# Attention and channel-mix kernel on one core: instruction order from a list schedule inside the kernel, shared PSUM banks, k and q transposed in fp32

## Chip, cores and metric

One core of a Trainium2 chip runs the kernel. The metric is the device time of one execution in microseconds (us). TensorE is PE below, VectorE DVE, ScalarE ACT, GpSimd POOL and SyncE SP.

## What is computed

Attention over 4 batches, 8 heads, 768 positions and 64 elements per head. A query sees its own and the 127 keys before it, and the first four keys of the sequence (the sinks). What comes out is the input x of a channel mix with two gates of its own:

```
scores = q @ k.T / 8, kept where 0 <= i - j < 128 or j < 4
a = softmax(scores);  x = a @ v                     # (4, 768, 512)
xk = mu_k * x + (1 - mu_k) * x_prev                 # x_prev: the position before
xr = mu_r * x + (1 - mu_r) * x_prev
out = sigmoid(xr @ w_r) * (relu(xk @ w_k) ** 2 @ w_v)
```

Inputs and output are fp32 (w_k 512x1024, w_v 1024x512, w_r 512x512); matmuls run in bf16.

## The kernel before, in words

The work is cut into 12 tiles of 256 positions (u = 0 to 11; three tiles, T = 0 to 2, make a batch). A tile goes through these steps, which the texts below call by these names:

- load: k, q and v of a tile. The first three tiles come as fp32 through SP's queue. From the fourth on, k and q are cast to bf16 on the way by DMAs that POOL issues (names kb, qb, L76); v stays fp32 (vs) and is cast by POOL (L179).
- preparation (`prepare`): four groups of four transposes each on PE (L172), k and q, two halves; ACT copies each group out of PSUM (L175).
- scores (L218) for each of four pairs of heads, exponential on ACT (L222), mask on DVE (L228, L231), values (L244, L255), division on DVE (L259, L260), which gives x. T > 0 has also a group of sink scores (L202).
- x transposed (L275), copied by ACT (L279), and mixed by DVE to xk and xr (L294, L298).
- the channel mix of a tile (`ffn`): eight key groups of four matmuls (L311) with relu on ACT and square on DVE, two gate groups (L323), four product groups (L331) with w_v, the last operation on DVE (L336) and the store (L339).

PE's order is written out by hand: a loop over n = 4u + c takes the pair c of tile u, and puts up to three pieces of an earlier tile's channel mix between its parts (`fill`). The other engines' order is made by the framework's scheduler. `idle` puts matmuls on zeros into PE's order in the first 18 us, 35 in all. PSUM has four pools: two banks for scores, two for transposes and sink scores, one for values, three for the channel mix. The weights come as fp32; POOL casts w_k and w_r to bf16 (L366, L369), DVE w_v (L372).

Of the kernel before, what the change touches and what calls it, by code (L numbers as in the profile page):

```python
# [8 lines left out]
FP32 = mybir.dt.float32  # L9
# [4 lines left out]
PSUM = bass.MemoryType.PSUM  # L14


@with_exitstack
def kernel(
# [14 lines left out]
    nc = tc.nc  # L33
# [25 lines left out]
    raw = {}  # L59

    def dtype(u, name):

        return FP32 if u < 3 or name == "v" else BF16

    def load(u, names="kqv", halves=1):
        b, T = divmod(u, NT)
        for name in names:
            if (u, name) not in raw:
                raw[u, name] = ld.tile([128, 2, H, D], dtype(u, name), name=name + ("s" if dtype(u, name) == FP32 else "b"))
        n = H // halves  # L70
        for i in range(halves):
            for name in names:
                for g in range(2):
                    s0 = 256 * T + 128 * g
                    ahead = dtype(u, name) != FP32
                    ins = (nc.gpsimd if ahead else nc.sync).dma_start(  # L76
                        out=raw[u, name][:, g, n * i:n * i + n, :],
                        in_={"k": k, "q": q, "v": v}[name][
                            b, n * i:n * i + n, s0:s0 + 128, :].rearrange("h p d -> p h d"))
                    if ahead:  # L80
                        tc.keep_in_program_order(ins)

    wk32 = const.tile([128, NC, Dff], FP32, name="wk32")
    wr32 = const.tile([128, NC, Dm], FP32, name="wr32")
    wv32 = const.tile([128, NF, Dm], FP32, name="wv32")
    with tc.manual_schedule(engines={mybir.EngineType.SP}):
        load(0, "kq", 2)
        load(0, "v")
        nc.sync.dma_start(out=wk32, in_=moe_w_k.rearrange("(c p) f -> p c f", p=128))
        load(1, "kq")  # L90
        nc.sync.dma_start(out=wr32, in_=moe_w_r.rearrange("(c p) f -> p c f", p=128))
        load(1, "v")
        nc.sync.dma_start(out=wv32, in_=moe_w_v.rearrange("(c p) f -> p c f", p=128))  # L93
        load(2)


    warm = const.tile([128, 512], BF16, name="warm")
    nc.vector.memset(warm, 0.0)
    ident32 = const.tile([128, 128], FP32, name="ident32")
    make_identity(nc, ident32)  # L100
    ident = const.tile([128, 128], BF16, name="ident")
    nc.gpsimd.tensor_copy(out=ident, in_=ident32)


    mask = const.tile([128, 2, 2, 2, 128], BF16, name="mask")
    mask0 = const.tile([128, 2, 3, 128], BF16, name="mask0")
# [9 lines left out]
    nc.gpsimd.memset(mask0, 1.0)  # L116
    keep(mask0[:, :, 0, :], "D")
    keep(mask0[:, :, 1, :], "U")
    keep(mask0[:, :, 2, :], "D")
    nc.gpsimd.memset(mask0[0:NS, :, 0:2, :], 1.0)  # L120

    wk_sb = const.tile([128, NC, Dff], BF16, name="wk_sb")
    wr_sb = const.tile([128, NC, Dm], BF16, name="wr_sb")
    wv_h = const.tile([128, NF, Dm], BF16, name="wv_h")
    mu_k_sb = const.tile([128, NC], FP32, name="mu_k_sb")
    nc.scalar.dma_start(out=mu_k_sb, in_=moe_mu_k.rearrange("(c p) -> p c", p=128))
    mu_r_sb = const.tile([128, NC], FP32, name="mu_r_sb")
    nc.scalar.dma_start(out=mu_r_sb, in_=moe_mu_r.rearrange("(c p) -> p c", p=128))

    nc.gpsimd.memset(mask, 1.0)  # L130
    for a in range(2):
        keep(mask[:, a, :, 0, :], "U")
        keep(mask[:, a, :, 1, :], "D")

    v_bufs = [const.tile([128, 2, H, D + 1], BF16, name=f"v{i}") for i in range(3)]
    for t in v_bufs:
        nc.gpsimd.memset(t[:, :, :, D:D + 1], 1.0)

    xts = [const.tile([128, NC, S + 2], BF16, name=f"xt{i}") for i in range(2)]
    for t in xts:  # L140
        nc.gpsimd.memset(t[:, :, 0:2], 0.0)

    ksink = [const.tile([128, NP * 136], BF16, name=f"ksink{i}") for i in range(2)]
    vsink = [const.tile([128, H, D + 1], BF16, name=f"vsink{i}") for i in range(2)]
    for t in ksink + vsink:
        nc.gpsimd.memset(t, 0.0)
# [337 lines left out]
```

## Time and profile before

| | |
|---|---|
| time, median of 3 runs | 205.57 us (205.5 to 205.82) |
| time of the profiled execution | 205.31 us |
| its span | 203.6 us |
| busy: PE, DVE, ACT, POOL | 180.9, 142.5, 125.2, 68.0 us |
| mean granted clock of PE | 0.966 |

The profile is of one execution. Its span runs from the first to the last instruction; its own time is 1.71 us longer. Busy time of PE counts matmuls from start to modelled end, and they overlap, so a busy PE is not PE at its peak. A clock of 1.00 is 2.4 GHz, 0.50 is 1.2 GHz.

### The profile page before, as it was taken

Reading aid. Unit: us, or ns where it says so; the run is one execution under the profiler, and the core shown is the slowest. Engines: PE = TensorE matmul, PEld = TensorE weight load, DVE = VectorE, ACT = ScalarE, POOL = GpSimd, SP = SyncE. Lnnn points to the kernel's source line nnn. Section 1 sums busy time; section 2 is a strip of 40 time slices with the busy share of each in tenths; the row PEclk is TensorE's granted clock in tenths of the full one; section 3 lists DMA queues with packets and bytes.
Section 4 is the critical chain, followed back from the end, with each engine's and each line's share of the span. In section 5 each row is a group of like instructions: output and inputs, shape, how many; then the busy total and the mean of one; then the engine's idle time right before and its main releaser. Section 6 shows DMA issues by size and latency. Waiting matters only on the chain.

```text
span 203.6 us, 4309 instructions
## 1 busy us (share of the span) xinstructions
PE 180.9 (89%) x1681; PEld 115.9 (57%) x1704; DVE 142.5 (70%) x345; ACT 125.2 (61%) x201; POOL 68.0 (33%) x106
## 2 busy tenths in 40 slices
PE   7976869853998999999998999999999999999992
PEld 2633636531584665665855656666647567566650
DVE  0079486950776995986878959858969688698731
ACT  2443527541586586795875785967857868756340
POOL 8947160172149922002389420031890000000000
PEclk9999669996699999999999999999999999999999
DMA  6999999879969999205299992002996011020202
GB/s 117 230 392 212 281 292 279 164 106 166 245 118 127 201 217 67 104 2 131 78 103 181 234 104 106 0 3 106 80 107 125 3 56 48 3 103 3 101 2 103
DMA packets 81572, 25.97 MB, mean 128 GB/s; under 512 B 76432, under 2 KB 76432, under 8 KB 81552
## 3 DMA queue, kind: packets, MB, share of 16 engines
q1 hardware_dynamic: 43056, 20.98, 41.2%
q0 software_dynamic: 37440, 4.72, 36.3%
q8 instruction: 13, 0.21, 0.4%
q10 hardware_dynamic: 1056, 0.00, 0.3%
q14 instruction: 7, 0.06, 0.1%
HBM read 24.12 MB, written 6.29 MB: 149 GB/s over the span
## 4 chain that ended last, share of the span: by engine, by line
PE 37%; DVE 20%; SPq 17%; DMA 10%; ACT 8%; issue 5%; POOL 2%; DVEq 0%; ACTq 0%
SPq L76 13%; PE mm L311 12%; DMA kb<-in_k_dram 8%; PE mm L323 8%; PE mm L331 7%; DVE o_sb L336 5%; DVE xk L298 5%; ACT e L222 4%; ACT kt L175 3%; DVE xr L298 2%; SPq L93 2%; DMA vs<-in_v_dram 2%; PE tps L172 2%; PE o L255 2%; DVE e L228 2%
## 5 line engine op out<-in xcount | busy, mean ns | idle before, releaser
L311 PE MATMUL mm<-xk,wk_sb 128*128 128x256 bf16 x384 | 52.1, 277 | 3.2 <-DVE xk L298 3.1
L222 ACT ACTIVATE e<-sc 128x1024 bf16<-128x1024 f32 (+1 forms) x48 | 45.9, 956 | 10.9 <-PE sc L218 10.1
L331 PE MATMUL mm<-wv_h,kk 128*128 128x512 bf16 x182 | 47.7, 385 | 1.0 <-DVE wv_h L372 0.3
L228 DVE TENSOR_TENSOR e<-e,mask 128x1024 bf16<-128x1024 bf16 x32 | 22.1, 690 | 28.9 <-ACT e L222 28.9
L315 ACT ACTIVATE rl<-mm 128x512 bf16<-128x512 f32 x48 | 28.9, 603 | 20.8 <-PE mm L311 17.6
L311 PEld LDWEIGHTS <-wk_sb 128*128 128x128 bf16 x384 | 35.2, 99 | 10.5 <-issue 5.0
L179 POOL CAST v<-vs 128x512 bf16<-128x512 f32 x24 | 18.5, 788 | 56.4 <-PE o L255 30.8
L298 DVE SCALAR_TENSOR_TENSOR xk<-td,mu_k_sb,xt 128x256 bf16<-128x256 bf16 x48 | 26.1, 578 | 0.0
L331 PEld LDWEIGHTS <-kk 128*128 128x128 bf16 x192 | 16.7, 99 | 14.0 <-issue 1.3
L323 PE MATMUL mm<-wr_sb,xr 128*128 128x512 bf16 x84 | 22.1, 380 | 0.7 <-issue 0.2
L298 DVE SCALAR_TENSOR_TENSOR xr<-td,mu_r_sb,xt 128x256 bf16<-128x256 bf16 x48 | 22.4, 499 | 0.0
L316 DVE TENSOR_TENSOR kk<-rl 128x512 bf16<-128x512 bf16 x48 | 20.0, 417 | 3.1 <-ACT rl L315 3.1
L255 PE MATMUL o<-v,e 128*128 128x65 bf16 x352 | 20.6, 194 | 1.1 <-DVE e L231 1.0
L255 PEld LDWEIGHTS <-e 128*128 128x128 bf16 x352 | 17.7, 98 | 5.9 <-DVE e L231 1.8
L260 DVE TENSOR_TENSOR x<-o,rec 128x256 bf16<-128x256 f32 x48 | 20.1, 420 | 0.7
L231 DVE TENSOR_TENSOR e<-e,mask 128x768 bf16<-128x768 bf16 x16 | 10.3, 641 | 14.8 <-ACT e L222 14.7
L336 DVE SCALAR_TENSOR_TENSOR o_sb<-th,mm 128x512 f32<-128x512 f32 x24 | 16.3, 679 | 4.0 <-PE mm L331 4.0
L175 ACT COPY kt<-tps 128x512 bf16<-128x512 bf16 x18 | 10.5, 583 | 13.9 <-PE tps L172 13.9
L218 PE MATMUL sc<-qt,kt 64*128 64x128 bf16 (+1 forms) x256 | 18.5, 244 | 0.0
L175 ACT COPY qt<-tps 128x512 bf16<-128x512 bf16 x18 | 10.5, 583 | 9.5 <-PE tps L172 9.5
L218 PEld LDWEIGHTS <-kt 64*128 64x128 bf16 x256 | 8.7, 95 | 13.3 <-issue 10.9
L76 POOL DMA_DIRECT2D qb<-in_q_dram x18 | 16.0, 907 | 0.0
(56 smaller groups left out, 211.4 us busy)
## 6 DMA issues: line engine op xcount, KB each, us to landing
vs<-in_v_dram SPq DMA_DIRECT2D x24, 256.0 KB, 5.2
out_dram<-o_sb SPq DMA_DIRECT2D x24, 256.0 KB, 2.0
kb<-in_k_dram POOLq DMA_DIRECT2D x18, 128.0 KB, 5.0
qb<-in_q_dram POOLq DMA_DIRECT2D x18, 128.0 KB, 5.8
wk<-in_moe_w_k_dram SPq DMA_DIRECT2D x1, 2048.0 KB, 9.4
wv<-in_moe_w_v_dram SPq DMA_DIRECT2D x1, 2048.0 KB, 13.6
ks<-in_k_dram SPq DMA_DIRECT2D x4, 256.0 KB, 10.1
qs<-in_q_dram SPq DMA_DIRECT2D x4, 256.0 KB, 5.9
```

What stands on the lines that cost most here:

```text
L76: ins = (nc.gpsimd if ahead else nc.sync).dma_start(out=raw[u, name][:, g, n * i:n * i + n, :], in_={"k": k, "q": q, "v": v}[name][b, n * ...
L175: nc.scalar.copy(out=dst[:, 2 * half:2 * half + 2, :, :], in_=ps)
L218: nc.tensor.matmul(out=sc[:, a, o0:o1], lhsT=lhs[rows], rhs=rhs[rows], start=True, stop=True)
L222: nc.scalar.activation(out=e[:, :, lo:], in_=sc[:, :, lo:], func=AF.Exp, scale=scale)
L228: nc.vector.tensor_tensor(out=e, in0=e, in1=mask.rearrange("p a g k q -> p a (g k q)"), op=ALU.mult)
L255: nc.tensor.matmul(out=o[:, g, a, :], lhsT=e[:, a, e0:e0 + 128], rhs=rhs, start=(T == 0 and i == 0), stop=(i == len(blocks) - 1), skip_gro ...
L298: nc.vector.scalar_tensor_tensor(out=dst[:, c0 + i, :], in0=td[:, i, :], scalar=mu[:, c0 + i:c0 + i + 1], in1=prv[:, i, :], op0=ALU.mult, ...
L311: nc.tensor.matmul(out=ps[:, i, :], lhsT=wk_sb[:, c, 128 * f:128 * f + 128], rhs=xk[:, c, :], start=(c == 0), stop=(c == NC - 1), skip_gro ...
L315: nc.scalar.activation(out=rl, in_=ps, func=AF.Relu)
L323: nc.tensor.matmul(out=ps, lhsT=xr[:, c, 128 * g:128 * g + 128], rhs=wr_sb[:, c, :], start=(c == 0), stop=(c == NC - 1))
L331: nc.tensor.matmul(out=ps, lhsT=kk[:, f, 128 * g:128 * g + 128], rhs=wv_h[:, f, :], start=(f == 0), stop=(f == NF - 1))
L336: nc.vector.scalar_tensor_tensor(out=o_sb, in0=th[g], scalar=1.0, in1=ps, op0=ALU.add, op1=ALU.mult)
```

## The change

A class `Plan` takes every operation of the kernel with its engine, an assumed length, what it reads and writes, which buffers it takes and holds, and a rank. `schedule` then goes through a model of the engines and always emits the operation that can start first; the rank decides between equals. All engines and SP's queue follow this order. Further: PSUM is one pool of six banks for all uses beside the two banks of scores; k and q of all tiles come as fp32 through SP's queue and are transposed in fp32 (no DMA is issued by POOL any more); DVE casts w_k and w_r; of the 35 idle matmuls 8 are left. The core of the diff:

```diff
+class Plan:
...
+    def op(self, engine, cost, emit, rank, reads=(), writes=(), take=(), hold=(), port=False,
+           lag=None, service=0.0):
+        self.ops.append(dict(engine=engine, cost=cost, emit=emit, rank=rank, reads=list(reads),
+                             writes=list(writes), take=list(take), hold=list(hold), port=port,
+                             lag=90.0 if lag is None else lag, service=service))
+
+    def schedule(self):
+        ops = self.ops
...
+            best = None
+            for engine, some in ready.items():
+                now = clock.get(engine, 0.0)
+                pick = None
+                for i in some:
+                    o = ops[i]
+                    t = max(now, at[i])
+                    if o["port"]:
+                        t = max(t, port.get("DVE" if engine == "POOL" else "POOL", 0.0))
+                    ok = True
+                    for name, _ in o["take"]:
+                        if not free[name]:
+                            ok = False
+                            break
+                        t = max(t, min(free[name])[0])
+                    if not ok:
+                        continue
+                    if pick is None or (t, o["rank"], i) < (pick[0], ops[pick[1]]["rank"], pick[1]):
+                        pick = (t, i)
+                if pick is None:
+                    continue
+                t0 = pick[0]
+                if best is None or t0 < best[0]:
+                    best = (t0, pick[1])
...
+            clock[o["engine"]] = t + o["cost"]
+            if o["port"]:
+                port[o["engine"]] = t + o["cost"]
+            end = t + o["cost"] + o["lag"]
+            if o["service"]:
...
-    ld = ctx.enter_context(tc.tile_pool(name="ld", bufs=3))
...
-    sc_ps = ctx.enter_context(tc.tile_pool(name="sc_ps", bufs=1, space=PSUM))
-    tr_ps = ctx.enter_context(tc.tile_pool(name="tr_ps", bufs=2, space=PSUM))
-    o_ps = ctx.enter_context(tc.tile_pool(name="o_ps", bufs=1, space=PSUM))
-    mm_ps = ctx.enter_context(tc.tile_pool(name="mm_ps", bufs=3, space=PSUM))
...
-        return FP32 if u < 3 or name == "v" else BF16
...
+    pool("sc", 1, [128, 2, 512], FP32, psum)
+    pool("bank", 6, [128, 512], FP32, psum)
...
-                    ins = (nc.gpsimd if ahead else nc.sync).dma_start(
...
+                    nc.sync.dma_start(
+                        out=buf[key][:, g, h0:h1, :],
+                        in_=src[b, h0:h1, s0:s0 + 128, :].rearrange("h p d -> p h d"))
...
+    for u in range(2, U):
+        load(u, "kqv", -92 if u == 2 else 10 * u - 18)
...
+    for i in range(4):
+        sl = slice(256 * i, 256 * i + 256)
+        P.op("DVE", dve(1024, 0.52), lambda sl=sl: nc.vector.tensor_copy(
+            out=wk_sb[:, :, sl], in_=wk32[:, :, sl]), 2 + i, reads=["wk32"], writes=[("wk", i)],
+            port=True)
+    for i in range(2):
+        P.op("DVE", dve(1024, 0.52), lambda i=i: nc.vector.tensor_copy(
+            out=wr_sb[:, 2 * i:2 * i + 2, :], in_=wr32[:, 2 * i:2 * i + 2, :]), 8 + i,
+            reads=["wr32"], writes=[("wr", i)], port=True)
+
...
+                        nc.tensor.transpose(
+                            out=ps[:, i, g, :],
+                            in_=src[:, g, 2 * c:2 * c + 2, :].rearrange("p a d -> p (a d)"),
+                            identity=ident if by else ident32)
+
+            P.op("PE", 250.0 if by else 450.0, transpose, rank + half, lag=PE_LAG,
+                 take=[("bank", psk)], reads=["ident" if by else "ident32"] + made, writes=[psk],
...
+                P.op("PE", 445.0, keys, rank + f2, lag=PE_LAG,
+                     take=[] if i else [("bank", psk)], hold=[("xk", u)] + ([psk] if i else []),
+                     reads=[("wk", f // 2)] + [("xk", u, c) for c in range(NC)] +
+                     ([psk + (0,)] if i else []), writes=[psk + (i,)])
...
+    idle(8, -200, ("idle", 0))
+    prepare(0, 0)
+    for u in range(U):
+        attend(u, 10 * u + 4)
+        if u + 1 < U:
+            prepare(u + 1, 10 * u + 11)
+        mix(u, 10 * u + 8)
+        if u > 0:
+            ffn(u - 1, 10 * u + FFN_AFTER)
+    ffn(U - 1, 10 * U + FFN_AFTER)
+    with tc.manual_schedule():
+        P.run()
...
-    def weights_k():
-        for i in range(4):
-            sl = slice(256 * i, 256 * i + 256)
-            nc.gpsimd.tensor_copy(out=wk_sb[:, :, sl], in_=wk32[:, :, sl])
-
-    def weights_rv():
-        nc.gpsimd.tensor_copy(out=wr_sb, in_=wr32)
-
-        for i in range(4):
-            nc.vector.tensor_scalar(out=wv_h[:, 2 * i:2 * i + 2, :],
-                                    in0=wv32[:, 2 * i:2 * i + 2, :],
-                                    scalar1=0.5, scalar2=None, op0=ALU.mult)
...
-                    prepare(u + 1, *PARTS[c])
```

In the rows below, lines of the changed kernel are its own: L395 prepares, L517 makes values, L598 key groups, L413 casts v, L354 casts w_k, L530 and L533 divide. The first of three places is PE's, where the preparation of the fourth tile begins. Before (kb_602 is k of tile 3, o_633 and e_533 are values of tile 2's first pair):

```order
L255 LDWEIGHTS e_533
L255 MATMUL o_633<-v1_157,e_533 128x65
L172 LDWEIGHTS kb_602
L172 MATMUL tps_648<-ident_135,kb_602 128x128
L172 LDWEIGHTS kb_602
L172 MATMUL tps_648<-ident_135,kb_602 128x128
L172 LDWEIGHTS kb_602
L172 MATMUL tps_648<-ident_135,kb_602 128x128
L172 LDWEIGHTS kb_602
L172 MATMUL tps_648<-ident_135,kb_602 128x128
L218 LDWEIGHTS kt_574
L218 MATMUL sc_658<-qt_581,kt_574 128x256
```

Now (ks0_68 and qs0_71 hold k and q of tile 3, e2_88 belongs to tile 2's third pair, xk1_101 to the channel mix of tile 1):

```order
L517 LDWEIGHTS e2_88
L517 MATMUL bank4_66<-vb2_118,e2_88 128x65
L517 LDWEIGHTS e2_88
L517 MATMUL bank4_66<-vb2_118,e2_88 128x65
L395 MATMUL bank0_62<-ident32_125,ks0_68 128x128 x4
L395 MATMUL bank1_63<-ident32_125,qs0_71 128x128 x4
L598 LDWEIGHTS wk_sb_137
L598 MATMUL bank3_65<-xk1_101,wk_sb_137 128x256
L598 LDWEIGHTS wk_sb_137
L598 MATMUL bank3_65<-xk1_101,wk_sb_137 128x256
```

The preparation of tile 3 has moved from behind the first pair of tile 2 to behind its third, amid the key groups of tile 1.

The second place is POOL's, from the cast of tile 1's v on. Before:

```order
L179 CAST v1_157<-vs_114 128x8x64 x2
L179 CAST v2_158<-vs_120 128x8x64 x2
L76 DMA kb_602<-in_k_dram 128x8x64 x2
L76 DMA qb_603<-in_q_dram 128x8x64 x2
L179 CAST v0_156<-vs_604 128x8x64 x2
L179 CAST v1_157<-vs_833 128x8x64
L185 COPY ksink1_167<-kt_647 64x4x4 x2
L76 DMA kb_831<-in_k_dram 128x8x64 x2
```

Now, from tile 0's v on:

```order
L413 CAST vb0_116<-vs0_74 128x8x64 x2
L426 COPY ksink0_131<-kt0_81 64x4x4 x2
L413 CAST vb1_117<-vs1_75 128x8x64 x2
L413 CAST vb2_118<-vs2_76 128x8x64 x2
L413 CAST vb0_116<-vs0_74 128x8x64 x2
L426 COPY ksink1_132<-kt0_81 64x4x4 x2
```

The DMA issues of k and q, which stood behind the casts of v, are gone.

The third place is DVE's, around the casts of w_k, at the end of tile 0's attention. Before:

```order
L259 RECIPROCAL rec_291<-o_284 128x4
L260 TENSOR_TENSOR x_260<-o_284,rec_291 128x2x128
L231 TENSOR_TENSOR e_281<-e_281,mask0_138 128x2x384
L259 RECIPROCAL rec_314<-o_307 128x4
L260 TENSOR_TENSOR x_260<-o_307,rec_314 128x2x128
L231 TENSOR_TENSOR e_304<-e_304,mask0_138 128x2x384
L192 TENSOR_TENSOR vsink0_168<-tps_334,hmask_174 32x8x64
L294 TENSOR_TENSOR td_330<-xt0_162 128x512
L259 RECIPROCAL rec_348<-o_341 128x4
L298 SCALAR_TENSOR_TENSOR xk_328<-td_330,mu_k_sb_147,xt0_162 128x256 x2
L260 TENSOR_TENSOR x_260<-o_341,rec_348 128x2x128
```

Now:

```order
L530 RECIPROCAL rec0_92<-bank0_62 128x4
L533 TENSOR_TENSOR x0_95<-bank0_62,rec0_92 128x2x128
L530 RECIPROCAL rec1_93<-bank1_63 128x4
L354 CAST wk_sb_137<-wk32_119 128x4x256 x4
L533 TENSOR_TENSOR x0_95<-bank1_63,rec1_93 128x2x128
L530 RECIPROCAL rec2_94<-bank2_64 128x4
L530 RECIPROCAL rec0_92<-bank3_65 128x4
L533 TENSOR_TENSOR x0_95<-bank2_64,rec2_94 128x2x128
L533 TENSOR_TENSOR x0_95<-bank3_65,rec0_92 128x2x128
L567 TENSOR_TENSOR td0_97<-xt0_129 128x512
```

Four casts of w_k stand between the first and second piece of tile 0's x. The two casts of w_r stand ten rows further on, ahead of the last piece of tile 0's xr.

## Rows read from the trace of the kernel before

**Rows 1.** The page's first part: busy time of each engine, share of the span, instructions

```profile
PE 180.9 (89%) x1681; PEld 115.9 (57%) x1704; DVE 142.5 (70%) x345; ACT 125.2 (61%) x201; POOL 68.0 (33%) x106
```

**Rows 2.** Stretches: length; PE, PEld, DVE, ACT, POOL busy; granted clock; DMA share; GB/s

```profile
45.00:54.00 9.00, 4.70 (x34) 2.78 (x36) 1.84 (x4) 2.05 (x4) 1.85 (x3) 0.64 1.59 188
54.00:86.16 32.16, 30.30 (x313) 20.13 (x314) 25.97 (x68) 23.34 (x39) 14.34 (x18) 1.00 1.20 148
86.16:127.92 41.76, 40.16 (x413) 26.57 (x418) 33.43 (x85) 30.71 (x51) 15.62 (x20) 1.00 0.89 115
127.92:169.68 41.76, 40.24 (x414) 26.54 (x418) 33.11 (x85) 30.71 (x51) 11.13 (x15) 1.00 0.51 65
169.68:203.60 33.92, 29.55 (x253) 18.57 (x254) 21.40 (x53) 16.85 (x27) 0.00 (x0) 1.00 0.13 47
```

**Rows 3.** Timeline of PE: start, length, work, [idle before it and releaser]

```profile
46.78 0.23 PE L172 MATMUL tps<-ident,kb 128*128 128x128 bf16 x1 [2.89 <-DMA kb<-in_k_dram]
49.53 0.50 PE L172 MATMUL tps<-ident,kb 128*128 128x128 bf16 x3 [2.52 <-DMA kb<-in_k_dram]
...
54.35 0.39 PE L311 MATMUL mm<-xk,wk_sb 128*128 128x256 bf16 x2
...
196.08 3.62 PE L331 MATMUL mm<-wv_h,kk 128*128 128x512 bf16 x16
```

**Rows 4.** Timeline of POOL and DVE: casts and DMA issues

```profile
40.34 0.85 POOL L179 CAST v<-vs 128x512 bf16<-128x512 f32 x1 [0.29 <-DMA vs<-in_v_dram]
41.14 1.90 POOL L76 DMA_DIRECT2D kb<-in_k_dram  x2
...
25.00 2.51 DVE L298 SCALAR_TENSOR_TENSOR xk<-td,mu_k_sb,xt 128x256 bf16<-128x256 bf16 x2
```

**Rows 5.** Timeline of PE: transposes of k/q from fp32, then from bf16

```profile
38.76 0.60 PE L172 MATMUL tps<-ident,ks 128*128 128x128 f32 x4
39.20 0.60 PE L172 MATMUL tps<-ident,qs 128*128 128x128 f32 x4
...
95.12 0.39 PE L172 MATMUL tps<-ident,qb 128*128 128x128 bf16 x4
95.34 1.03 PE L331 MATMUL mm<-wv_h,kk 128*128 128x512 bf16 x4
```

**Rows 6.** Timeline of PE: one piece of the steady stage

```profile
89.18 0.62 PE L202 MATMUL tps<-qt,ksink 128*128 128x256 bf16 x4
89.73 0.39 PE L218 MATMUL sc<-qt,kt 64*128 64x256 bf16 x6
90.06 1.04 PE L323 MATMUL mm<-wr_sb,xr 128*128 128x512 bf16 x4
90.93 0.22 PE L244 MATMUL o<-vsink,es 128*128 128x130 bf16 x1
...
91.29 1.03 PE L331 MATMUL mm<-wv_h,kk 128*128 128x512 bf16 x4
92.15 0.39 PE L172 MATMUL tps<-ident,kb 128*128 128x128 bf16 x4
```

**Rows 7.** The load of w_v: its issue, its landing, and the casts behind it

```profile
20.09 4.70 SPq L93 DMA_DIRECT2D wv<-in_moe_w_v_dram  x1
...
DMA to landing us min/median/max: 13.6/13.6/13.6
...
35.78 2.49 DVE L372 TENSOR_SCALAR wv_h<-wv 128x1024 bf16<-128x1024 f32 x4
```

**Rows 8.** Timeline of PE and ACT: a score group; a relu and the exponential

```profile
42.17 0.39 PE L218 MATMUL sc<-qt,kt 64*128 64x256 bf16 x6
...
33.07 0.60 ACT L315 ACTIVATE rl<-mm 128x512 bf16<-128x512 f32 x1 [0.54 <-PE mm L311]
...
42.61 1.02 ACT L222 ACTIVATE e<-sc 128x1024 bf16<-128x1024 f32 x1
```

More of the change, by code (lines that the diff above doesn't have):

```diff
@@ L83 @@
[L83 to L94, printed above, removed]
@@ L97, with emit @@
[L97 to L106, printed above, removed]
+            src = {"k": k, "q": q, "v": v}[name]
+            for g in range(2):
+                s0 = 256 * T + 128 * g
+                def emit(key=(name, u), src=src, g=g, s0=s0):
+                    nc.sync.dma_start(
+                        out=buf[key][:, g, h0:h1, :],
+                        in_=src[b, h0:h1, s0:s0 + 128, :].rearrange("h p d -> p h d"))
+                rows = 128 * (h1 - h0)
+                first = g == 0 and h0 == 0
+                P.op("SP", rows * 0.9 + 60.0, emit, rank, service=rows * 1.19 + 60.0,
+                     take=[(name + "s", (name, u))] if first else (),
+                     hold=() if first else [(name, u)],
+                     writes=[(name, u, g, hp) for hp in range(h0 // 4, (h1 + 3) // 4)])
@@ L126 @@
[L126 to L146, printed above, removed]
-    hmask = const.tile([32, H, D + 1], BF16, name="hmask")
-    nc.gpsimd.memset(hmask, 1.0)
-    nc.gpsimd.affine_select(out=hmask, in_=hmask, compare_op=ALU.is_ge, fill=0.0, base=0,
-                            pattern=[[-4, H], [0, D + 1]], channel_multiplier=1)
@@ new lines, in make_mask, with make_ones, make_edges @@
+    def make_mask():
+        nc.gpsimd.memset(mask, 1.0)
+        for a in range(2):
+            keep(mask[:, a, :, 0, :], "U")
+            keep(mask[:, a, :, 1, :], "D")
+    const_op("POOL", 2300.0, make_mask0, ["mask0"], rank=-55)
+    def make_ones():
+        for t in P.pools["vb"]:
+            nc.gpsimd.memset(t[:, :, :, D:D + 1], 1.0)
+    const_op("POOL", 400.0, make_ones, ["ones"], rank=-54)
+    xts = [tile1([128, NC, S + 2], BF16, f"xt{i}") for i in range(2)]
+    def make_edges():
+        for t in xts:
+            nc.gpsimd.memset(t[:, :, 0:2], 0.0)
@@ L281, in mix @@
-    def mix(u, half, which):
+                nc.gpsimd.tensor_copy(out=kz[rows, :, 4 * a:4 * a + NS],
+                                      in_=buf["kt", u][rows, :, 0, 0:NS])
+        P.op("POOL", 500.0, sink_keys, rank + 4, hold=[("kt", u)], port=True,
+             reads=["sinks", ("kt", u, 0), ("kt", u, 1)], writes=[("ksink", b % 2)])
+        psk = ("vsp", b)
+        P.op("PE", 250.0, lambda: nc.tensor.matmul(
+            out=buf[psk].rearrange("p (h d) -> p h d", h=H), lhsT=spread,
+            rhs=buf["vb", u][:, 0, :, 0:D], start=True, stop=True), rank + 4, lag=PE_LAG,
+            take=[("bank", psk)], hold=[("vb", u)], reads=["spread", ("vb", u, 0)], writes=[psk])
@@ L283, in mix @@
+    def mix(u, rank):
         b, T = divmod(u, NT)
         xt = xts[b % 2]
[L285 removed]
         t0 = 2 + 256 * T
[L287 to L295 removed]
@@ L342, in stream @@
-    def stream():
-        for u in range(U):
-            yield from ffn(u)
-    chunks = stream()
-    N = U * NP
-    FIRST = {4: 2, 5: 2, 6: 2, 7: 2, 8: 1, 9: 1}
-    def fill(count):
-        for _ in range(count):
-            next(chunks, None)
-    def idle(count, width=512):
-        ps = mm_ps.tile([128, 512], FP32, name="mm")
-        for _ in range(count):
-            nc.tensor.matmul(out=ps[:, 0:width], lhsT=warm[:, 0:128], rhs=warm[:, 0:width],
-                             start=True, stop=True)
@@ new lines, in idle, with emit @@
+    def idle(count, rank, key):
+        def emit():
+            for _ in range(count):
+                nc.tensor.matmul(out=buf[key], lhsT=warm[:, 0:128], rhs=warm, start=True,
+                                 stop=True)
+        P.op("PE", 220.0 * count, emit, rank, take=[("bank", key)], reads=["warm"], lag=PE_LAG)
+    idle(8, -200, ("idle", 0))
[7 more added lines that the diff above has]
+            ffn(u - 1, 10 * u + FFN_AFTER)
```

655 lines of the change are left out of this document (398 added, 257 removed).

## Prediction

> **What bounds the kernel now.** I read the page first. PE is busy 180.9 of 203.6 us, DVE 142.5, ACT 125.2, POOL 68.0 [rows 1]. A share over the whole span hides stages, so I cut the span into stretches. From 54 us on PE is busy 30.30 of 32.16 us, then 40.16 and 40.24 of 41.76 (three tiles each, 13.92 us a tile), at granted clock 1.00, while DVE is busy 33 of 41.76 [rows 2]. PE is the bound there: from 54 us to its last matmul it idles only 1.86 + 1.60 + 1.52 us and 0.47 in the last stretch (33.92 - 29.55, less the 3.9 us that follow PE's last matmul), 5.45 us in all. Between 45 and 54 us it is otherwise: PE is busy 4.70 of 9 us, and the clock is 0.64 on average [rows 2], that is at 1.2 GHz for most of it. PE's timeline says what it waited for: twice, 2.89 and 2.52 us, the group that transposes k of tile 3, released by the DMA of kb [rows 3]. That DMA was late at its issue: POOL casts v of tile 2, which lands at 40.34 us, and issues kb only behind that cast, at 41.14 us [rows 4]. Products of the first channel mix were ready, but stood behind the transposes in PE's order. So there are two parts: a start that data and orders hold up, and a PE-bound remainder, which begins when the key groups of tile 1's channel mix begin, at 54.35 us, and ends at 196.08 + 3.62 = 199.70 us [rows 3]. That is 145.35 us; with 54.35 before and 3.9 behind (last DVE operation, store, end) it makes the span of 203.6.
>
> **The start, step by step.** Loads up to v of tile 2 keep their order on SP, so I keep their landings. w_v is issued at 20.09 and lands 13.6 us later, at 33.7 [rows 7]. The changed kernel has nothing on PE that waits for tile 3 at this point: k and q of tile 3 follow v of tile 2 directly on SP, without POOL, and their transposes stand behind three pairs of tile 2 and six key groups. What holds PE up is then w_v. Its casts take 2.49 us for four on DVE [rows 7], 0.62 each, and the first product group needs two of them: 33.7 + 1.24 = 35.0 us with the release. From that product group to the first key group of tile 1 the new order has on PE four product groups (0.86 each, 91.29 to 92.15), four fp32 preparations (0.44, below), one values group (0.36, 90.93 to 91.29), two score groups (0.33, 89.73 to 90.06), a sink group (0.55, 89.18 to 89.73) [rows 6] and one transposition of x (0.22, as four other bf16 transposes took, 95.12 to 95.34 [rows 5]): 3.44 + 1.76 + 0.36 + 0.66 + 0.55 + 0.22 = 7.0. So the key groups begin at 42.0 us at the earliest. In between, x of tile 1's last pair has to go through DVE, PE and ACT into xk, and the casts of w_v stand ahead of that mask on DVE. I estimate 2 us of waits from this chain and take 44 us; if the clock is at 1.2 GHz through these 7.0 us they double, and with some waiting it is up to 47 us.
>
> Before w_v, PE has to be done with tile 0's key groups. DVE casts w_k and w_r now, six casts of about 0.62 us, 3.7 us together. They cost x of tile 0 its early place: the second piece of x waits for w_k and its four casts. But the step that ended this stage before was the mixing, where two operations took 2.51 us on DVE while POOL was casting w_r [rows 4]; those POOL casts are gone. I count these two against each other and the key groups of tile 0 as done by 35 us. The missing 27 idle matmuls cost nothing in the sum as they stood where PE waited for data; the cover that they gave the clock is what the 47 us above allows for.
>
> **The rest, step by step.** At its start the new order has left open what the old one had done: one score group (0.33), two values groups (0.72) and two preparations (0.44): 1.5 us. Then the transposes. Four fp32 ones took 0.44 us start to start at full clock (38.76 to 39.20), four bf16 ones 0.22 (95.12 to 95.34) [rows 5]: 0.22 us more per group, four groups in each of nine tiles, 36 x 0.22 = 7.9 us, on the engine that is the bound. Nothing covers this. POOL's 36 issues go, and with them the time in which DVE and POOL meet; DVE has room either way, so I give nothing for it. Six shared banks and the list order act on PE's 5.45 us of idle time alone. An order from assumed lengths can win these or add to them. The lengths written in the plan are close to the rows (a preparation 0.45 against 0.44, a product group 0.87 against 0.86), so I take half of them as won, 2.7 us; the bounds are all of it, and none.
>
> Sum: 44 + 145.35 + 1.5 + 7.9 - 2.7 + 3.9 = 199.95 us of span, against 203.6. The profiled execution took 1.71 us beside its span, and the median of the runs is 0.26 above that execution: 199.95 + 1.97 = **201.9 us**. With the early start (42) and all idle time won it is 197.2, with the late one (47) and none won 207.6.
>
> One rule speaks against the transposes. In the rows above a transpose from fp32 takes twice the bf16 time, 0.11 against 0.055 us. The Trainium skill, in FP8 and Floating Point Precision, TensorE Precision Notes, says that true FP32 goes through the PE array in four passes. By that rule a group would take 4 x 0.22 = 0.88 us, 36 groups would add 23.8 instead of 7.9 us, and the sum would be 217.8. The trace does not agree for transposes, so this is a rival with hardly a chance.
>
> **The rivals.**
> First, a start that gains less: PE finishes tile 0's key groups and gates, then waits for w_v, and the clock falls to 1.2 GHz as it did behind the wait for kb, so that the key groups of tile 1 begin at 47 us or later. For it: PE has 0.64 of the clock in the stretch after a wait of some 5 us [rows 2, 3], and most idle matmuls are gone. Against: PE would have to wait about as long, and tile 1's scores and values fill in. With half the idle time won: 204.9 us, about no change.
>
> Second, slower: the scores. They have one buffer, so a score group waits until the exponential of the last one is done: start of scores to end of the exponential is 42.61 + 1.02 - 42.17 = 1.46 us [rows 8], and a release on top. The new order puts three key groups (0.43 each, half a product group, since their matmuls are half as wide) behind one score group, 1.29 + 0.33 = 1.62 us, but only two and a values group behind the next, 0.86 + 0.36 + 0.33 = 1.55; and a relu, 0.60 us [rows 8], stands on ACT between two exponentials. If each of these two exponentials is late by a relu, PE stands still about 1 us a tile, 10 us over ten tiles: 201.9 + 10 = 212; from 0.4 us a tile on, the gain of 3.7 us is gone. Against: PE idles only some 0.5 us a tile now, with ACT busy 30.7 of 41.76 us [rows 2].
>
> Third, faster than the forecast: the early start, and nearly all idle time won, 197 to 199 us. For it: the assumed lengths agree with the rows. Against: orders fixed ahead meet landings and collisions that the plan only assumes.
>
> Fourth, four passes per fp32 transpose as above: 217.8 us.
>
> **How the numbers follow.** The forecast (200 to 204) has 0.46, the third 0.22, the first 0.12, the second 0.18, the fourth 0.02. The range leaves out the far ends of the second and the third: 197.5 to 206.5. A measurement of this kernel tells from no change about 0.2%, 0.4 us. Faster than 205.16 are the forecast, the third, and half of the first: 0.74. The same: half of the first, 0.06. Slower: the second and the fourth, 0.20.
>
> **What would show it.** Right, if in the new profile no PE wait names the loads of tile 3, the key groups of tile 1 begin between 42 and 46 us, a group of fp32 transposes takes 0.44 us in the steady stage, and three tiles take 41.8 to 43.5 us there instead of 41.76. Wrong in its first step, if PE waits for w_v or its casts for more than 3 us with the clock at 0.5 behind it. Wrong in its last, if the steady stage shows PE waiting for exponentials or masks, three tiles taking over 45 us, or under 41.5, where the transposes would have cost less than their rows say.

## The result, and the profile after

The changed kernel takes 196.94 us (median of 4 runs, 195.76 to 198.69), the kernel before 205.69 in the runs beside it: ratio 0.955, interval 0.947 to 0.962. That is faster, by 8.75 us where 3.7 were forecast, and 0.6 us below the forecast range. Ratios leave out the runs of a kernel that lie more than 1.5% above its fastest, medians do not, so the two can differ. The profiled execution of the changed kernel is the slowest of its four, 198.69 us, with a span of 197.0.

The first part of its page stands against [rows 1]: PE has the same busy time in a span 6.6 us shorter, POOL less than half.

```profile
PE 180.6 (92%) x1676; PEld 122.1 (62%) x1676; DVE 148.8 (76%) x351; ACT 124.4 (63%) x201; POOL 29.7 (15%) x65
```

PE's timeline of the changed kernel at the places of [rows 3, 5, 7]: the wait for k of tile 1, the wait for w_v, the preparation of tile 3, and the last product groups.

```profile
18.19 0.47 PE L395 MATMUL bank<-ident,ks 128*128 128x128 f32 x1 [4.42 <-DMA ks<-in_k_dram]
...
35.08 2.63 PE L636 MATMUL bank<-wv_h,kk 128*128 128x512 bf16 x8 [2.56 <-DVE wv_h L363]
...
44.65 1.48 PE L598 MATMUL bank<-xk,wk_sb 128*128 128x256 bf16 x12
...
49.44 0.63 PE L395 MATMUL bank<-ident,ks 128*128 128x128 f32 x4
49.90 0.60 PE L395 MATMUL bank<-ident,qs 128*128 128x128 f32 x4
50.34 0.60 PE L598 MATMUL bank<-xk,wk_sb 128*128 128x256 bf16 x4
...
189.62 3.62 PE L636 MATMUL bank<-wv_h,kk 128*128 128x512 bf16 x16
```

The two waits for kb, 5.4 us, are gone; nothing waits at tile 3. Four fp32 transposes take 0.44 to 0.46 us start to start. The key groups of tile 1 begin at 44.65 us (44 forecast), and PE ends at 193.24.

To compare stages I take as a mark the sink scores of a tile, one group at the head of its attention (L202 before, L449 now). Tile 4's stand at 75.35 us before and at 68.81 now, those of tiles 7 and 10 three tiles further on each. The stretches of the changed kernel between the marks of tiles 2, 4, 7, 10 and 11, and from there to the end, with the columns of [rows 2]:

```profile
43.13:68.81 25.68, 25.09 (x255) 17.76 (x252) 23.55 (x59) 20.23 (x33) 5.93 (x9) 1.00 1.08 218
68.81:111.37 42.56, 42.56 (x419) 29.15 (x418) 36.38 (x87) 30.62 (x50) 4.93 (x8) 1.00 0.97 212
111.37:153.93 42.56, 42.56 (x419) 29.16 (x418) 36.00 (x86) 30.63 (x50) 4.07 (x7) 1.00 0.30 74
153.93:168.47 14.54, 14.54 (x150) 10.19 (x149) 9.51 (x24) 10.36 (x17) 0.00 (x0) 1.00 0.10 38
168.47:197.00 28.53, 24.46 (x201) 14.94 (x199) 17.48 (x41) 12.15 (x20) 0.00 (x0) 1.00 0.15 56
```

And two of the same stretches of the kernel before:

```profile
75.35:117.11 41.76, 40.15 (x412) 26.59 (x417) 33.42 (x86) 30.72 (x51) 15.62 (x20) 1.00 0.89 114
117.11:158.88 41.77, 40.26 (x412) 26.55 (x417) 33.12 (x86) 30.73 (x51) 12.17 (x16) 1.00 0.66 77
```

Up to tile 4's mark 6.54 us are won. Then the new kernel is slower: 85.12 us for six tiles against 83.53 (+1.59), 14.54 against 13.83 for the next (+0.71). From tile 11's mark to PE's end it takes 24.77 us, the kernel before 26.99 (172.71 to 199.70): it has less work left, which it did ahead of tile 4. By tile 4's mark it has run four matmuls of products, four of gates, four transposes of x and six matmuls of values more than the old order (counted in e5 below, whose trace is complete), 2.1 us at their slots. Sum: -6.54 + 1.59 + 0.71 - 2.22 = -6.46, PE's end moving from 199.70 to 193.24. So between these two executions, which lie 6.6 us apart, 8.8 us are won ahead of tile 4, and 2.3 of them are given back. That the difference of the medians is 8.75 has nothing to do with this 8.8.

One thing about the rows before has to be put right. In the steady stage they have 412 matmuls for three tiles, the rows after 419. The work is the same; the view that groups instructions, for the kernel before, shows what is missing:

```profile
L331 PE MATMUL mm<-wv_h,kk 128*128 128x512 bf16 x182 | 47.7, 385 | 1.0 <-DVE wv_h L372 0.3 <-issue 0.2
L323 PE MATMUL mm<-wr_sb,xr 128*128 128x512 bf16 x84 | 22.1, 380 | 0.7 <-issue 0.2
```

Twelve tiles have 192 product and 96 gate matmuls; 22 records are missing, 20 of them behind 54 us (167 and 77 are there, 176 and 88 run). Little of the idle time comes from them. A record of these forms lasts 0.38 us, and the next one starts 0.217 us later, so the records beside a missing one leave a gap of 2 x 0.217 - 0.385 = 0.05 us. The trace has 20 gaps of that size behind 54 us, 1.05 us in all, and 16 longer ones, 4.4 us. So 4.4 of the 5.45 us that the prediction called idle are real waits; those between the marks of tiles 4 and 10 are (place, releaser, us in total, times, longest):

```profile
PE tps L275 <- ACT kt L175: 0.9, 2, 0.4
PE tps L275 <- DVE x L260: 0.7, 4, 0.2
PE mm L311 <- DVE xk L298: 0.7, 2, 0.5
PE tps L172 <- DMA kb<-in_k_dram: 0.2, 1, 0.2
```

The changed kernel has no wait in this stage: PE is busy 42.56 of 42.56 us in the rows above.

### The profile page after: what moved, and what is told of

Its sections match the earlier page's. It is cut to its first block, busy times and chain, and to the rows that moved or that the text cites. A ratio compares the mean times of both kernels' runs of the same rounds, so it can differ in the third digit from the quotient of the medians.

```text
span 197.0 us, 4325 instructions
## 1 busy us (share of the span) xinstructions
PE 180.6 (92%) x1676; PEld 122.1 (62%) x1676; DVE 148.8 (76%) x351; ACT 124.4 (63%) x201; POOL 29.7 (15%) x65
## 4 chain that ended last, share of the span: by engine, by line
PE 78%; SPq 10%; DMA 7%; DVE 1%; issue 1%; ACT 1%; DVEq 0%
PE bank L636 21%; PE bank L598 21%; PE bank L395 10%; PE bank L621 10%; SPq L237 9%; DMA wv<-in_moe_w_v_dram 7%; PE sc L476 6%; PE bank L517 5%; PE bank L556 3%; PE bank L505 2%; PE bank L449 1%; SPq L248 1%; ACT e L484 1%; DVE xk L577 0%; DVE ob L645 0%
## 5 line engine op out<-in xcount | busy, mean ns | idle before, releaser
L598 PE MATMUL bank<-xk,wk_sb 128*128 128x256 bf16 x384 | 53.8, 273 | 0.3 <-DVE xk L577 0.2
L636 PE MATMUL bank<-wv_h,kk 128*128 128x512 bf16 x192 | 49.2, 383 | 2.6 <-DVE wv_h L363 2.6
L493 DVE TENSOR_TENSOR e<-e,mask 128x1024 bf16<-128x1024 bf16 (+1 forms) x48 | 32.0, 670 | 16.4 <-ACT e L484 16.4
L598 PEld LDWEIGHTS <-wk_sb 128*128 128x128 bf16 x384 | 34.5, 98 | 8.5 <-issue 1.6
L607 ACT ACTIVATE rl<-bank 128x512 bf16<-128x512 f32 x48 | 28.2, 609 | 5.0 <-PE bank L598 4.3
L413 POOL CAST vb<-vs 128x512 bf16<-128x512 f32 x24 | 16.7, 710 | 78.4 <-PE bank L517 43.0
L577 DVE SCALAR_TENSOR_TENSOR xr<-td,mu,xt 128x256 bf16<-128x256 bf16 x48 | 24.3, 530 | 0.0
L621 PE MATMUL bank<-wr_sb,xr 128*128 128x512 bf16 x96 | 23.5, 379 | 0.0
L577 DVE SCALAR_TENSOR_TENSOR xk<-td,mu,xt 128x256 bf16<-128x256 bf16 x48 | 23.1, 502 | 0.5
L395 PE MATMUL bank<-ident,ks 128*128 128x128 f32 x96 | 17.6, 309 | 5.3 <-DMA ks<-in_k_dram 5.3
L517 PE MATMUL bank<-vb,e 128*128 128x65 bf16 x352 | 20.8, 197 | 0.1
L533 DVE TENSOR_TENSOR x<-bank,rec 128x256 bf16<-128x256 f32 x48 | 20.0, 421 | 0.7
L517 PEld LDWEIGHTS <-e 128*128 128x128 bf16 x352 | 18.0, 100 | 2.3 <-issue 0.2
L395 PEld LDWEIGHTS bank<-ident,ks 128*128 128x128 f32 x96 | 12.5, 158 | 7.8 <-DMA ks<-in_k_dram 6.4
```

Source lines behind the costliest of these rows:

```text
L395: nc.tensor.transpose(out=ps[:, i, g, :], in_=src[:, g, 2 * c:2 * c + 2, :].rearrange("p a d -> p (a d)"), identity=ident if by else ident32)
L493: nc.vector.tensor_tensor(out=buf[ek][:, :, lo:], in0=buf[ek][:, :, lo:], in1=m, op=ALU.mult)
L517: nc.tensor.matmul(out=o[:, g, a, :], lhsT=e[:, a, e0:e0 + 128], rhs=rhs, start=(T == 0 and i == 0), stop=(i == len(blocks) - 1), skip_gro ...
L533: P.op("DVE", dve(256), lambda ok=ok, rk=rk, c=c: nc.vector.tensor_tensor(out=buf["x", u][:, :, 128 * c:128 * c + 128].rearrange("p g (a d ...
L577: nc.vector.scalar_tensor_tensor(out=buf[key][:, c0 + i, :], in0=buf[tk][:, i, :], scalar=mu[w][:, c0 + i:c0 + i + 1], in1=xt[:, c0 + i, t ...
L598: nc.tensor.matmul(out=ps[:, i, :], lhsT=wk_sb[:, c, 128 * f:128 * f + 128], rhs=xk[:, c, :], start=(c == 0), stop=(c == NC - 1), skip_gro ...
```

## The experiments

Times are medians; a kernel's executions differ by 1 to 7 us, those of the kernel before most (201.2 to 208.8), so kernels of one set are compared. Sets: 1 is e1 to e4 (before: 204.99), 2 is e5, e6, e8, c1 (204.44), 3 is e7, e9, e10, e12 (204.88), 4 is f1 to f3, c2 (205.31).

**One part of the change in the old order.** e1: k and q of all tiles in fp32 by SP's queue.

```diff
-        return FP32 if u < 3 or name == "v" else BF16
+        return FP32
```

> The kernel before with one part of the change: k and q of all tiles come as fp32 through SP and are transposed in fp32; PE's order and the PSUM pools stay. Theory S (start and price): POOL's late issue goes, the hole at tile 3 shrinks (k of tile 3 is now issued behind the first store on SP, at some 42 us), and each of 36 groups of transposes costs 0.22 us more on PE, 7.9 us: the two cancel, 202 to 207 us. Rival F (fp32 transposes are nearly free on a PE that idles anyway): 197 to 201 us.

Measured: 203.09 us, ratio 0.996 (0.991 to 1.000). PE's timeline at tile 3, and the six tiles from tile 4's mark on:

```profile
46.40 0.30 PE L172 MATMUL tps<-ident,ks 128*128 128x128 f32 x1 [1.34 <-DMA ks<-in_k_dram]
47.51 0.55 PE L172 MATMUL tps<-ident,ks 128*128 128x128 f32 x3 [0.81 <-DMA ks<-in_k_dram]
```

```profile
72.64:115.48 42.84, 42.29 (x412) 29.06 (x417) 33.50 (x87) 30.66 (x50) 5.92 (x10) 1.00 1.00 203
115.48:158.02 42.54, 41.99 (x412) 29.06 (x417) 32.81 (x87) 30.62 (x50) 5.02 (x8) 1.00 0.40 96
```

The hole shrinks from 5.4 to 2.15 us. And the old order with fp32 takes 85.38 us for six tiles, as long as the new one (85.12). So in the steady stage the list schedule wins 0.3 us over the old order with the same operations, and the 24 fp32 groups cost 1.85 us net, 0.08 each, where 0.22 was taken. What covers the rest are the waits of the kernel before: of its nine in this stage, 2.5 us, e1 has two left.

```profile
PE tps L275 <- ACT kt L175: 0.5, 2, 0.2
```

Summed from start to start of the matmuls, the transposes of k and q take 4.8 us more than before in these six tiles, and key groups, transposes of x and scores 2.9 us less. PE's order is the same in both. That POOL issues no DMA in e1 may have part in it; this is not separated.

e2: bf16 as before, but the preparation of tile 3 behind the third tile's last pair.

```diff
-                if u == 1:
+                if u in (1, 2):
                     if c == 3:
                         for part in PARTS:
-                            prepare(2, *part)
-                        cast_values(2)
+                            prepare(u + 1, *part)
+                        cast_values(u + 1)
+                        if u == 2:
+                            sink_keys(1)
```

> The kernel before with only PE's order around tile 3 changed: its four preparations and its casts stand behind the fourth pair of tile 2, not one behind each pair; loads stay with POOL. Theory S: PE has products and key groups before it while k lands, most of the 5.4 us of waiting and the 1.2 GHz behind it go, 198 to 201 us. Rival L (the gain of the change comes from the list order and shared banks in the steady stage, not from the hole): the hole moves or is filled with nothing, 204 to 206 us.

Measured: 203.49 us, ratio 1.002 (0.996 to 1.008): nothing. The wait moved on by one tile, to kb of tile 4:

```profile
59.03 0.23 PE L172 MATMUL tps<-ident,kb 128*128 128x128 bf16 x1 [1.26 <-DMA kb<-in_k_dram]
60.60 0.42 PE L172 MATMUL tps<-ident,kb 128*128 128x128 bf16 x3 [1.34 <-DMA kb<-in_k_dram]
```

POOL issues these loads in turn behind casts, so a later preparation finds the next load late. e5 makes both edits:

> The kernel before with both edits: all k and q as fp32 through SP, and tile 3 prepared behind the fourth pair of tile 2; old order elsewhere. Theory S (the gain of the change is the start, less the price of the fp32 transposes, and the order wins back most of that price): no wait for k of tile 3 or 4, the sink group of tile 4 comes at some 69 us as in the changed kernel, then 42.8 us per three tiles as with fp32 in the old order: 198.5 to 201 us. Rival M (the hole only moves on to the next late thing, as it did when the order alone was mended): 202 us and up. Rival L (the start gives nothing): 204 us and up.

Measured: 201.67 us, ratio 0.991 (0.986 to 0.996), with no listed wait for a load of tiles 3 or 4. The hole, mended in both its causes, is worth 2 to 3 us (1.8 by the ratio, 2.8 by the medians), the price of the fp32 transposes already taken off. The changed kernel in the same set, c1, took 195.28:

> The changed kernel once more, on the chip of the three kernels beside it: a base for them. 195 to 199 us; sink group of tile 7 follows that of tile 4 by 42.5 us, as in the first trace of it.

6.4 us lie between them. Both profiled executions take the same for six tiles (85.24 and 85.12 us); c1 reaches tile 4's mark at 66.22 us against 68.55, and has 2.2 us less left at tile 11's. The stretch from 40 us to tile 4's mark, with nearly the same number of matmuls, first e5, then c1:

```profile
40.00:68.55 28.55, 26.23 (x261) 17.84 (x259) 20.74 (x55) 19.75 (x32) 4.57 (x8) 1.00 0.93 188
40.00:66.22 26.22, 25.65 (x260) 17.98 (x258) 24.25 (x60) 20.60 (x34) 5.85 (x10) 1.00 1.08 228
```

PE is without work for 2.32 us there in e5 and for 0.57 in c1, both at full clock. That is three quarters of the 2.33 us at tile 4's mark. Up to 40 us c1 has run 235 matmuls of the work, e5 211. e9 asks whether e5's further idle matmuls are the gap. They are 28: the code of the kernel before has 36, one more than its trace shows and the texts ahead say. e9 is e5 with 8 at its head:

```diff
-        idle(10)
+        idle(8)
...
-            idle(4)
```

> The old order with its start mended (all k and q in fp32 by SP's queue, preparation of tiles 2 and 3 late), and now with 8 idle matmuls at its head where it had 35. Theory: the rest of the gap to the changed kernel (201.67 against 195.28 us) is not the 27 idle matmuls, since they lie ahead of k of tile 1, whose load ends the wait at about 18 us with or without them; then the time stays within 1 us of 201 us, and it may be slower by up to 2 us where the granted clock falls. Rival: they take 5 us of PE that real work could have; then 197 us or less.

Measured: 201.88 us, so no. f2 is e9 with the four product groups of tile 0 ahead of the preparation of tile 2:

```diff
-    FIRST = {4: 2, 5: 2, 6: 2, 7: 2, 8: 1, 9: 1}
+    FIRST = {4: 2, 5: 2, 6: 2, 7: 4}
...
+                        if u == 1:
+                            fill(count - 2)
                         for part in PARTS:
...
-            fill(count - 2)
+            if n != 7:
+                fill(count - 2)
```

> The old order with its start mended and 8 idle matmuls (201.88 us), and now all four product groups of the first tile ahead of the preparation of the third tile, as the changed kernel has them. Theory: what is left of the gap is PE waiting at small places of the start (0.79 us for q of the third tile, 0.46 us for its copy, and others) while work that could run stands behind; with the products ahead these go and 1 to 2 us are won: 200 to 201 us. Rival: the same waits come back a pair later, where no piece is left to fill with; within 0.6 us of 201.9 us.

Measured: 203.71 us (200.51 to 205.60), no gain. Its waits (place, releaser, us in total, times, longest) show what came instead:

```profile
PE mm L311 <- DVE xk L298: 2.9, 3, 1.3
PE o L255 <- POOL v L179: 2.3, 2, 1.3
PE tps L172 <- DMA ks<-in_k_dram: 2.2, 2, 1.8
PE o L255 <- DVE x L260: 2.1, 3, 1.2
```

Many small waits, for xk, x and v, stand in its start. None of these edits of the old order reaches the changed one.

**One part of the change undone.** e3 and e6 keep the new order, but POOL casts k and q to bf16 and PE transposes bf16: e3 for all tiles, e6 from tile 3 on, e10 from tile 2 on.

```diff
-CAST = {"k": None, "q": None}
+CAST = {"k": "POOL", "q": "POOL"}
...
-            by = CAST[name]
+            by = CAST[name] if u >= 3 else None
```

> The changed kernel with k and q of all tiles cast to bf16 by POOL (four casts a tile) and transposed in bf16; the schedule is made anew from that. Theory S: each of 48 groups saves 0.22 us on PE, 10.6 us, of which the first two tiles are hidden by the start: 187 to 190 us. Rival F (the fp32 price is not on the path): 195 to 198 us. Rival P (the casts of POOL and the operations of DVE block each other): over 199 us.

Measured: 194.55 us, ratio 0.955 (0.949 to 0.961). PE waits 8.9 us for POOL's casts in the start, but six tiles take 81.55 us instead of 85.12:

```profile
69.71:110.49 40.78, 39.97 (x415) 26.07 (x417) 37.80 (x87) 30.53 (x51) 17.37 (x24) 1.00 1.09 242
110.49:151.26 40.77, 40.06 (x415) 26.19 (x417) 36.91 (x86) 30.14 (x50) 10.85 (x16) 1.00 0.15 49
```

In the new order, then, a fp32 group costs 3.57 / 24 = 0.15 us more than a bf16 one. And with bf16 six tiles take 2.0 us less in the new order than in the old one (83.53), where POOL's DMAs did the casting. This fits an order that wins more where no longer transposes fill the waits, but the two also load k and q in different ways.

> The changed kernel with k and q of tiles 3 to 11 cast to bf16 by POOL and transposed in bf16; tiles 0 to 2 stay fp32. Theory S: the start of the changed kernel, then 40.8 us per three tiles as with all tiles cast: 1.7 us per three tiles less than now, 190 to 193 us, faster than the changed kernel and than the version with all tiles cast. Rival P (POOL's casts delay v or DVE in the start of tile 3): 194 us and up.

Measured: 192.79 us, ratio 0.939 (0.925 to 0.953), against 195.28 for c1 in its set.

> The changed kernel with k and q cast to bf16 by POOL from the third tile on (u of 2 and more) and transposed in bf16; the first two tiles stay fp32. From the fourth tile on it gave 192.79 us. Theory: a bf16 group of transposes takes 0.15 us of PE less, and four groups more give 0.6 us: 192 to 193.5 us. Rival: k of the third tile is needed while POOL still casts v behind a late load, PE waits for the casts as it did with all tiles in bf16: 194 us or more.

Measured: 195.53 us (192.69 to 196.64), in another set than e6: what the third tile's casts cost or give is not to be told from this.

e4 splits the six banks into the old shares: two for transposes and sink scores, one for values, three for the channel mix.

```diff
-    pool("bank", 6, [128, 512], FP32, psum)
+    pool("tps", 2, [128, 512], FP32, psum)
+    pool("ops", 1, [128, 512], FP32, psum)
+    pool("mm", 3, [128, 512], FP32, psum)
```

> The changed kernel with the six shared banks split as before: two for transposes and sink scores, one for values, three for the channel mix; the schedule is made anew. Theory S: the idle time that was won comes from the order, not from the banks, 196 to 199 us. Rival B (the shared banks win it): 3 us or more slower than the changed kernel, 200 us and up.

Measured: 198.91 us, ratio 0.976 (0.969 to 0.983), 2 us more than the changed kernel's median beside the result. No unchanged copy of it ran in this set, so how much the shared banks win is not told exactly. Its waits have two that the changed kernel lacks or has shorter:

```profile
PE ops L519 <- DVE x L535: 2.0, 2, 1.7
PE mm L600 <- DVE xk L579: 1.8, 3, 1.1
```

e12 casts w_k on POOL again.

```diff
-        P.op("DVE", dve(1024, 0.52), lambda sl=sl: nc.vector.tensor_copy(
+        P.op("POOL", gps(1024), lambda sl=sl: nc.gpsimd.tensor_copy(
```

> The changed kernel with the four casts of w_k on POOL again, as in the kernel before, instead of DVE. Theory: the first key group is ended by xk at about 24 us, and POOL's casts, 1.2 us each from 17 us on, end at about 22 us; so nothing is lost: within 0.6 us of the changed kernel, and the chain up to the landing of w_v is the same. Rival: DVE's faster casts of w_k (0.63 us each) are what lets the start be as short as it is; then 1.5 us or more is lost, with a PE wait for w_k.

Measured: 196.26 us, within the spread of the changed kernel. Which engine casts w_k makes no difference that shows.

e7 counts every operation as 400 ns in the schedule.

```diff
+        cost = cost if engine == "SP" else 400.0
```

> The changed kernel, but the schedule counts every operation of PE, DVE, ACT and POOL as 400 ns long, whatever it is; the rules, the ranks, the loads' lengths, the banks and all operations stay. Theory: the time that PE no longer waits is won because the model's lengths resemble those on the chip, so that a matmul group is put where its operands are just ready; with flat lengths PE waits again. Then three tiles take 43.5 us or more (42.56 in the changed kernel), PE is idle for over 1 us of each such 42 us, and the time is 200 us or more. Rival: the dependences, the ranks and six banks give a good order with any lengths; then 42.4 to 43.0 us for three tiles and 195 to 197.5 us.

Measured: 199.84 us, ratio 0.979 (0.966 to 0.991), 3.6 us above e12 in its set (3.0 by the ratios). Three tiles take 42.84 and 43.27 us, and tile 4's mark stands at 68.24 against 65.47 in e12. Between the two theories: dependences and ranks alone give more than half of the gain, the lengths the rest, and most of that in the start, not in the steady stage.

**The wait for w_v, and the clock.** c1's executions lie 1.7 us below those of the first set of runs, c2's 1.0 above:

> The changed kernel, unchanged, as a measure for the three beside it. Its runs so far lay between 195.27 and 198.69 us; 195 to 198.7 us. Three tiles take 42.56 us.

Measured: 197.91 us (195.45 to 198.84). The profiled execution of 198.69 us against c1's, 196.08, in the same two stretches. First the longer one, then c1:

```profile
36.00:40.00 4.00, 4.00 (x25) 2.96 (x23) 3.64 (x10) 0.59 (x1) 0.03 (x1) 0.57 1.08 218
40.00:45.00 5.00, 4.43 (x41) 2.87 (x39) 4.06 (x9) 3.70 (x7) 1.21 (x2) 1.00 1.06 196
```

```profile
36.00:40.00 4.00, 4.00 (x39) 3.06 (x38) 3.82 (x10) 2.27 (x5) 0.62 (x1) 1.00 1.24 237
40.00:45.00 5.00, 4.43 (x60) 3.26 (x58) 4.72 (x11) 3.92 (x6) 0.62 (x1) 1.00 1.08 209
```

Behind the wait for w_v the granted clock is 0.57 in the one, most of it at 1.2 GHz, and 1.00 in the other: 25 matmuls in four busy microseconds against 39. Tile 2's mark stands at 43.13 against 40.74 us. From there to PE's end both take 150 us (150.11 and 149.91). Of the 2.4 us between the marks 0.9 are the later end of the wait (35.08 against 34.22), the other 1.5 the clock behind it. The first rival's mechanism is there, in some executions. In c1 the key groups of tile 1 begin at 42.26 us:

```profile
42.26 1.48 PE L598 MATMUL bank<-xk,wk_sb 128*128 128x256 bf16 x12
```

e8 puts 16 idle matmuls behind tile 0's values.

```diff
+        if u == 0:
+            for i in range(4):
+                idle(4, 100, ("idle", 1 + i), [("o", 0, 3)])
```

> The changed kernel with 16 idle matmuls put into PE's order behind the values of tile 0, where PE waits some 4.4 us for k of tile 1. Theory C (part of the time, and of the spread between executions, is the clock at 1.2 GHz in the first 45 us): granted clock of 20 to 25 us goes up, the runs lie within 1 us of each other, median 1 to 2 us under the changed kernel's. Rival: the load of w_v ends the wait there in any case, no change of the median over 0.5 us.

Measured: 197.46 us against 195.28 for c1. Its clock is 1.00 from 25 to 45 us, but PE still waits 2.83 us for w_v: filling the earlier wait does not shorten this one. Its first cast of w_v began 1.3 us later than c1's (34.78 against 33.47 us); whether the filler has part in that is not shown. f1 loads w_v in four pieces, so that the first casts start early:

```diff
-    load_weight(wv32, moe_w_v, "wv32", 5200.0, -93)
+    for i in range(4):
+        load_weight(wv32[:, 2 * i:2 * i + 2, :], moe_w_v[256 * i:256 * i + 256, :], ("wv32", i),
+                    1300.0, -93)
```

> The changed kernel with the load of w_v in four pieces, each cast on its own. In the changed kernel DVE's first cast of w_v waits 2.4 us for the whole load and PE then 2.2 us for the cast (at 34 us). Theory: PE's wait there is a cost of its own; with the first quarter there some 3 us earlier it is gone, and the time falls by 1.2 to 2.5 us. Rival: the loads as a whole hold the start (k and q of the third tile come behind w_v); then PE waits for k of the third tile instead, and the time stays within 0.6 us.

Measured: 194.48 us (194.03 to 195.96), ratio 0.948 (0.941 to 0.956). That is 3.4 us below c2's median; by the ratios, 0.948 and 0.955, it is 1.3 us, and between the profiled executions of f1 and c1 1.9 us. So 1 to 2 us are shown, as forecast. f1's executions also spread less than c2's (2 against 3.4 us); whether the edit is the reason, four runs do not tell. DVE's casts, and PE's first product group:

```profile
28.55 0.69 DVE L365 TENSOR_SCALAR wv_h<-wv 128x1024 bf16<-128x1024 f32 x1 [0.16 <-DMA wv<-in_moe_w_v_dram]
29.88 0.69 DVE L365 TENSOR_SCALAR wv_h<-wv 128x1024 bf16<-128x1024 f32 x1
```

```profile
30.33 1.24 PE L638 MATMUL bank<-wv_h,kk 128*128 128x512 bf16 x4
```

PE no longer waits there, the clock stays at 1.00 from 25 us on, and no wait for k of tile 2 takes its place. f3 joins this edit and e6's:

> The changed kernel with k and q cast to bf16 by POOL from the fourth tile on (192.79 us when it ran alone with that), and w_v loaded in four pieces. Theory: both gains add up, 190 to 192 us, three tiles 40.6 to 42.2 us. Rival: the start's gain is eaten by k and q of the third and fourth tile, which then come late: 192.5 us or more.

Measured: 189.58 us (188.97 to 192.24), ratio 0.922 (0.916 to 0.927): faster than c2 by 8.3 us in the medians and 6.9 by the ratios, most of what the change itself won. The two gains add up at least: by the ratios they are 1.3 (f1 against c2) and 4.4 us (e6 against c1) by themselves.

## Why the prediction was wrong

The sum's terms against the profiled execution: the start 44 us forecast, 44.65 measured; the rest 152.05 (145.35 + 1.5 + 7.9 - 2.7), 148.59 measured (193.24 - 44.65); the tail 3.9 and 3.76; beside the span 1.71 and 1.69. So 201.66 forecast for an execution like the profiled one, 198.69 measured: 2.97 too high. And the median lies 1.75 below that execution where 0.26 above was added: 2.0 more. Together the 4.96 between 201.9 and 196.94.

- **The start: the hole as forecast, the sum near, in part by luck.** The hole goes because tile 3 is no longer waited for at that place. e1 and e2 show that it takes both parts: the later place alone moves the wait to tile 4, the SP queue alone leaves 2.15 us. The prediction named POOL's issue and the place of the group, and both are causes. The first product group came at 35.08 us, 35.0 forecast, because two errors cancel: the first cast of w_v began at 34.33 where 33.7 was taken, and PE began 0.75 us behind its start where two casts were counted, 1.24. And the 2 us of waits from x to xk behind it did not come: PE has one wait there, 0.57 us for an exponential, and the clock took the rest. In c1, at full clock, the key groups begin at 42.26, close to the prediction's "earliest" 42.0.
- **The step that failed is "The rest, step by step": it charged the transposes in full, 7.9 us, with "Nothing covers this", and took only half of PE's idle time, 2.7 us, as won.** Forecast 5.2 us net. The 0.22 us per group is right as a duration: in the changed kernel a group takes 0.44 to 0.46 us. But PE's waits do cover it: in e1, with the old order kept, they fall from 2.5 to 0.5 us in six tiles, and 24 groups cost 1.85 us instead of 5.3. Of the 5.45 us only 1.05 were gaps of missing records. The longer transposes fill most of the real waits, so the list order has little left to win there. 36 groups at e1's net price are 2.8, and the order wins a few tenths more. That is 2.7 of the 3.46 us by which the rest came out lower; the remaining 0.8 are not taken apart.
- **The offset** from one execution to the median, the other 2.0 us, came out as it did because the profiled execution is the slowest of four. The prediction held 0.4 us to be a difference that can be told; the executions of the kernel before differ by over 6 us within one set.
- **The first rival, a start that gains less,** describes what happens in some executions, at a smaller price: a wait for w_v of 2.6 us, then 0.57 of the clock, and 1.5 us lost by it. It is part of why the offset had the wrong sign; how large a part, the profiles of so few executions do not tell.
- **The second, slower by waiting for exponentials,** did not come about: the steady stage shows no PE wait that the views list, with the one buffer for scores. All waits of scores for an exponential are in the start, 2.6 us in four.
- **The third was nearest, in time and in mechanism.** Its start at 42 us came in c1 (42.26), and in the steady stage nothing of PE's idle time is left. With the transposes in full and all 5.45 us of idle time won, the rest is 149.3 us, and 148.6 were measured. What it had differently is who wins the idle time: e1 shows that the longer transposes do most of it without the new order.
- **The fourth:** the Trainium skill (FP8 and Floating Point Precision, TensorE Precision Notes) counts four passes for true FP32. Four transposes of 128x128 took 0.44 us here, twice the bf16 time, in the new order too; four passes are not seen for transposes.

Of what would show it, the key groups of tile 1 between 42 and 46 us, no wait for tile 3, 0.44 us a group and three tiles in 41.8 to 43.5 us (42.56) all came true. The sum itself made the three tiles 43.6 (41.76, 2.64 for twelve groups, less 0.8 of the 2.7), just outside its own sign.

What stays open is which parts of the list schedule win the 4 to 6 us between e5 and c1. The stretch from 40 us on shows 1.75 us less waiting, and 2.1 us of work are done earlier; c1 has 11.2 us of PE without work up to tile 4's mark, e5 10.3 and 28 more idle matmuls (some 6 us at their slots). Taking those out (e9) or filling one place (f2) did not win it; e7 says that part of it hangs on the lengths in the plan, and e4 suggests that the banks have a part.

## What to carry to other kernels

Before idle time is called a wait or a hole in the record, look at each gap: 20 missing matmuls made 1.05 us of idle time here, the other 4.4 us were waits. A longer operation on the bound engine costs less than its length where that engine waits between its operations, and idle time that it fills cannot be won by the order again. So take both from a stage that is changed in this alone, not from one row each. And where a wait is at the first use of a large load, split the load before adding filler work: that won 1 to 2 us here, filler none.

## What the hardware showed beside

Executions of the same kernel differ in the first 45 us: in two of the changed kernel w_v's first cast began 0.9 us apart (33.47 and 34.33 us), but the clock behind it turned this into 2.4 us. The length of the wait does not decide it alone: after 2.52 and 2.56 us the clock fell, after 2.22 and, in e8, 2.83 us it did not.
